# Where the first q is loaded: a GpSimd queue shared by q, k and v, or hardware queues with the cast on VectorE

## The chip, the core and the metric

The kernel runs on one core of a Trainium2 chip. A core has five engines that run side by side, each with its own instruction stream: TensorE (PE, matrix products), VectorE (DVE), ScalarE (ACT), GpSimd (POOL) and SyncE (SP, which here only issues transfers). They meet through semaphores. Data moves between the chip's memory (HBM) and the core's working memory (SBUF) by DMA: an engine issues a transfer, sixteen DMA engines carry it, and a semaphore tells when it has landed. PE writes its results to PSUM, from which DVE or ACT copies them.

The metric is the time of one execution on the device in microseconds (us); lower is better. A profile is one execution with every instruction recorded; its span runs from the first instruction to the last.

## The reference

Linear attention with decay, then a two-layer network with an ELU between. `lam` has one decay per head.

```python
def _attn_ref(q, k, v, lam):                      # q, k, v: (4, 8, 768, 64) float32
    block = 64
    ...
    for b in range(S // block):
        intra = einsum('bhic,bhjc->bhij', qb, kb) * Dmask      # lam ** (i - j), 0 above the diagonal
        intra = einsum('bhij,bhjd->bhid', intra, vb)
        inter = einsum('bhid,bhde->bhie', qb * lam_pow, kv_state)
        out[:, :, sl] = intra + inter
        kv_state = lam_block * kv_state + einsum('bhsd,bhse->bhde', kb * rev_pow, vb)

def _moe_ref(x, w_in, w_out):                     # x: (3072, 512); w_in: 512 x 2048; w_out: 2048 x 512
    h = x @ w_in
    g = where(h > 0, h, exp(min(h, 0)) - 1)
    return g @ w_out
```

## The kernel before

Everything is computed in half precision (FP16) with sums in float. The 3072 tokens are 24 chunks of 128: chunk g is block g // 4 of batch g % 4, so chunks 0 to 3 are the first 128 tokens of the four batches, and they have no earlier state. For a chunk, attention runs over all 8 heads, which are held as 4 pairs (`HP`), two heads of 64 on 128 partitions. The network works on tiles of 4, 2, 4, 4, 4, 4 and 2 chunks (`TS`). The order of the work on each engine is written out by hand; the Tile layer below only adds the semaphores.

**Attention of one chunk.** q and k arrive with tokens on partitions. PE turns them so that the head dimension lies on partitions (`att_T`, L223) and ACT copies the result from PSUM (`att_Te`, L235). PE makes the scores (`att_S`, L310), DVE multiplies them with the decay mask (`att_mask`, L322), PE multiplies with v (`att_O`, L336; for chunk 3 `att_OX2`, L267, in two halves) and ACT copies the result into `xt`, the network's input (`att_X`, L363; `att_OX2`, L272). Later chunks also use and update a state (`att_kd`, `att_U`, `att_st`), with factors `ks`, `up` and `qs`, and with the mask `mask1` in place of `mask`.

**The masks.** `mask` (chunks 0 to 3) is exp(lag x log lam) per head, eight ACT instructions at L172, times a causal matrix (DVE, L175). `mask1` is the causal matrix times `dn` (DVE, L163). ACT loads one table of functions for the logarithm of lam and another for exp.

**The network.** For a tile, `mm1` forms 16 column blocks n of 128 (L443; L461 for tiles of two chunks), ACT makes exp and relu (L472, L476), DVE joins them to `g` (L489, or L484 and L487 for three blocks of the first tile), `mm2` sums over the 16 blocks (L540), and the result is copied and stored (L557; the last chunk by `mm2_last`, L520 to L527). The first tile's stage A is `mm1` with n = 0 to 15, with first `mm2` products between; stage B is the rest of its `mm2`, with attention of chunks 4 and 5 between. From then on the network of one tile and attention of the next are interleaved to the end.

**The loads.** All loads of q, k, v and the weights convert float to half on the way, and are issued by POOL, in the order of the list `LOADS` (`emit_load` L74, `emit_wi` L99, `emit_wo` L106). A load of one chunk's q, k or v writes 128 KB to SBUF, in rows of one token of one head (64 floats in HBM, 64 halves in SBUF). `wi` is loaded in eight pieces of 1, 1, 2, 2, 2, 2, 2 and 4 blocks n, `wo` in five. Two of the entries are no loads but the product `kd` of chunks 0, 1 and 2, 3, which POOL computes (L297) between its issues; it needs `ks`. At most eight of POOL's loads are in flight with one semaphore each: the ninth waits for the first to land. SP issues the load of `lam` (L52), the transposing copies of later chunks (L279) and most stores (L557); those of chunks 18 and 19 are POOL's.

**The opening** (chunks 0 to 3, up to stage A) is the straight list L591 to L645. `warm(k)` (L568) puts in products of ones whose results nobody reads; they keep PE busy while it waits.

Of the kernel before, what the change touches and what calls it, by code (L numbers as in the profile page):

```python
# [7 lines left out]
FP32 = mybir.dt.float32  # L8
FP16 = mybir.dt.float16
I32 = mybir.dt.int32  # L10
AF = mybir.ActivationFunctionType
ALU = mybir.AluOpType
# [3 lines left out]
def kernel(  # L16
# [34 lines left out]
    lam_b = cpool.tile([128, H], FP32, name="lam_b")  # L51
    nc.sync.dma_start(out=lam_b[:], in_=lam.unsqueeze(0).broadcast_to([128, H]))  # L52
    rel_i = cpool.tile([128, 128], I32, name="rel_i")
# [60 lines left out]
    ]  # L114
    LOADS = [(0, 1, 'q'), (0, 1, 'k'), (1, 1, 'q'), (1, 1, 'k'), (2, 1, 'q'), (2, 1, 'k'), (3, 1, 'q'), (3, 1, 'k'), (0, 1, 'v'), (1, 1, 'v'), (2, 1, 'v'), (3, 1, 'v'), ('wi', 0), ('wi', 1), ('wi', 2), ('wi', 3), ('wi', 4), ('kd', 0), ('wi', 5), ('wi', 6), ('wo', 0), ('wi', 7), ('kd', 2), ('wo', 1), ('wo', 2), (4, 2), ('wo', 3), ('wo', 4), (6, 2), (8, 2), (10, 2), (12, 2), (14, 2), (16, 2), (18, 2), (20, 2), (22, 2)]

    def run_loads(items):
        for it in items:
            if it[0] == "wi":
                emit_wi(it[1])  # L120
            elif it[0] == "wo":
                emit_wo(it[1])
            elif it[0] == "kd":
                att_kd(it[1], 2, "p")
            else:
                emit_load(*it)

    run_loads(LOADS[:0])
    nc.gpsimd.iota(rel_i[:], pattern=[[1, 128]], base=0, channel_multiplier=-1)
    run_loads(LOADS[0:16])  # L130

# [27 lines left out]
    dn = cpool.tile([128, H], FP32, name="dn")  # L159
    nc.scalar.activation(dn[:], loglam[:], AF.Exp, scale=pos[:, 0:1])  # L160
    mask1 = cpool.tile([128, 2, HP, 128], FP32, name="mask1")
    for hh in range(2):
        nc.vector.tensor_tensor(  # L163
            out=mask1[:, hh],
            in0=causT[:].unsqueeze(1).broadcast_to([128, HP, 128]),
            in1=dn[:, hh::2].unsqueeze(2).broadcast_to([128, HP, 128]),
            op=ALU.mult,
        )

    def build_mask0(hh):  # L170
        for h in range(hh, H, 2):
            nc.scalar.activation(  # L172
                mask[:, hh, h // 2, :], lag[:], AF.Exp, scale=loglam[:, h : h + 1]
            )
        nc.vector.tensor_tensor(  # L175
            out=mask[:, hh], in0=mask[:, hh],
            in1=causT[:].unsqueeze(1).broadcast_to([128, HP, 128]), op=ALU.mult,
        )

    build_mask0(0)  # L180
    ks = cpool.tile([128, H], FP32, name="ks")
# [27 lines left out]
    def att_T(g, n, which, tag="S"):  # L209

        j = "qk".index(which)
        if n == 1:
            t1 = ps.tile([128, 1, HP, 128], FP16, tag=tag, bufs=2, name=f"psT{which}{g}")
            pT[g, j] = t1[:]
        elif j == 0:
            t2 = ps.tile([128, 2, n, HP, 128], FP16, tag=tag, bufs=2, name=f"psT{g}")
            pT[g, 0], pT[g, 1] = t2[:, 0], t2[:, 1]
        pt = pT[g, j]
        ts = (qn, kn)[j]
        for i in range(n):  # L220
            nat = heads(ts, g + i)
            for hp in range(HP):
                nc.tensor.transpose(  # L223
                    pt[:, i, hp, :], in_=nat[:, 2 * hp : 2 * hp + 2, :],
                    identity=ident16[:],
                )

    def att_Te(g, n, which, eng):
        j = "qk".index(which)
        pt = pT.pop((g, j))  # L230
        dst = asb.tile([128, n, HP, 128], FP16, tag=f"{which}T", name=f"{which}T{g}", bufs=4)
        if eng == "v":
            nc.vector.tensor_copy(dst[:], pt)
        else:
            nc.scalar.copy(out=dst[:], in_=pt)  # L235
        for i in range(n):
            (qT, kT)[j][g + i] = dst[:, i]

    def att_T2(g, which, tag):
# [112 lines left out]
    def att_X(g, n, parts=1):  # L352
        t, i = where[g]
        if i == 0:
            xt[t] = asb.tile([128, HP, TS[t] * L], FP16, tag="xt", name=f"xt{t}")
        po = pS.pop(("O", g))
        w = HP // parts
        for j in range(parts):
            c = slice(j * w, (j + 1) * w)
            dst = xt[t][:, c, i * L : (i + n) * L].rearrange("p h (n l) -> p n h l", n=n)  # L360
            if g < B:
                copy = nc.vector.tensor_copy if g in () else nc.scalar.copy
                copy(out=dst, in_=po[:, :, c])  # L363
                continue
            nc.vector.tensor_tensor(  # L365
                out=dst, in0=po[:, :, c],
                in1=qs[:, c].unsqueeze(1).broadcast_to([128, n, w, 128]),
                op=ALU.mult,
            )

    def att_U(g, tag="S"):
# [160 lines left out]
    def mm2(t, i, n, tag="M"):  # L532
        if T0[t] + i == NG - 1:
            if n == NF - 1:
                mm2_last(t, i)
            return
        if n == 0:
            psM[t, i] = ps.tile([128, DM], FP32, tag=tag, bufs=2, name=f"psM{t}_{i}")
        pm = psM[t, i]
        nc.tensor.matmul(  # L540
            pm[:], lhsT=gt[t][:, n, i * L : (i + 1) * L],
            rhs=wo_t[wo_at[n][0]][:, wo_at[n][1], :], start=(n == 0), stop=(n == NF - 1),
        )
        if n < NF - 1:
            return
        c, b = divmod(T0[t] + i, B)
        t0 = b * S + c * L
        o = msb.tile([128, DM], FP32, tag="osb", bufs=6, name=f"osb{t}_{i}")
        last = T0[t] + i == NG - 1
        if last:  # L550
            raise AssertionError
        else:
            if i % 2:
                nc.vector.tensor_copy(o[:], pm[:])
            else:
                nc.scalar.copy(o[:], pm[:])  # L556
            (nc.gpsimd if T0[t] + i in (18, 19) else nc.sync).dma_start(  # L557
                out=out[t0 : t0 + L, :], in_=o[:]
            )
        psM.pop((t, i))  # L560

    def warm(k, tag="M"):
        if k <= 0:
            return
        pw = ps.tile([128, 4, 128], FP32, tag=tag, bufs=2, name=f"psW{len(warms)}")
        warms.append(pw)
        for w in [4] * (k // 2) + [2] * (k % 2):
            nc.tensor.matmul(  # L568
                pw[:, 0:w], lhsT=ones[:], rhs=any16[:, 0:w], start=True, stop=True
            )  # L570
# [13 lines left out]

    def op_T(c, w):
        att_T(c, 1, w, "H")

    def op_Te(c, w):
        att_Te(c, 1, w, "a")

    W = [14, 6, 2, 2, 2, 0, 2, 0, 4, 0, 0, 2, 0, 2, 0, 0, 4, 0, 0, 0, 0]  # L591
    warm(W[0])
    op_T(0, "q")
    op_Te(0, "q")
    build_mask0(1)
    warm(W[1])
    op_T(0, "k")
    op_Te(0, "k")
    warm(W[2])
    op_T(1, "q")  # L600
    op_Te(1, "q")
    att_S(0)
    att_mask(0, 2)
    warm(W[3])
    op_T(1, "k")
    op_Te(1, "k")
    late_ks()
    warm(W[4])
    op_T(2, "q")
    op_Te(2, "q")  # L610
    att_S(1)
    att_mask(1, 2)
    warm(W[5])
    op_T(2, "k")
    op_Te(2, "k")
    late_up()
    warm(W[6])
    op_T(3, "q")
    op_Te(3, "q")
    att_S(2)  # L620
    att_mask(2, 2)
    late_qs(0, 1)
    warm(W[7])
    op_T(3, "k")
    op_Te(3, "k")
    cut, ecut = {}, {}
    for x, f in zip([('O', 0), ('S', 3), ('qs', 0), ('O', 1), ('qs', 1), ('O', 2), ('qs', 2), ('qs', 3), ('O2', 3, 'S'), ('L', 0, 384)], W[8:]):
        warm(f, "M" if not cut else "S")
        if x[0] == "O":
            att_O(x[1], 1, "M" if x[1] < 2 or not cut else "S")  # L630
            att_X(x[1], 1)
        elif x[0] == "S":
            att_S(x[1])
            att_mask(x[1], 2)
        elif x[0] == "qs":
            late_qs(x[1], x[1] + 1)
        elif x[0] == "O2":
            att_OX2(x[1], x[2])
        elif x[0] == "L":
            lo = cut.get(x[1], 0)  # L640
            mm1_mm(0, x[1], lo, x[2], "M" if x[1] % 2 == 0 else "H")
            cut[x[1]] = x[2]
        elif x[0] == "E":
            elu_cols(0, x[1], 0, cut[x[1]], x[2])
            ecut[x[1]] = cut[x[1]]  # L645

    run_loads(LOADS[16:29])
    for s, g in zip([], (0, 2)):
# [45 lines left out]

    for s, a, b in [(('B', 2), 29, 30), ((1, 2), 30, 31), ((1, 14), 31, 32), ((2, 4), 32, 33), ((2, 12), 33, 34), ((3, 4), 34, 35), ((3, 12), 35, 36), ((4, 4), 36, 37)]:
        at(s, paced_load, s, LOADS[a:b])
# [52 lines left out]
```

## Time and profile before

| | us |
|---|---|
| median of 3 runs (212.57 to 212.66) | 212.57 |
| the profiled execution | 212.6 |
| its span | 210.8 |
| PE busy | 203.6 |
| DVE busy | 148.4 |
| ACT busy | 128.0 |
| POOL busy | 62.4 |
| L540, second matmul, 368 products | 94.0 |
| L443, first matmul, 324 products | 81.4 |

The span is 1.8 us shorter than the execution that it belongs to. A line such as `L443 PE MATMUL psH<-xt,wi` reads: line 443 of the kernel, on PE, writes psH and reads xt and wi. Matmuls overlap in the pipeline, so the time of one alone is longer than the step from one to the next; the step is what counts in a row of them. "PEld" is PE's weight load, which runs beside its products. In a list of the timeline the first number is the start from the span's beginning and the second the length, and what stands in brackets is the idle time before and what ended it. The transfer engines' share counts packets in flight, so it may be over 1. Transfers before, by the page (count, KB written by each, median us from issue to landing):

```profile
qn<-in_q_dram POOLq DMA_DIRECT2D x4, 128.0 KB, 4.5
kn<-in_k_dram POOLq DMA_DIRECT2D x4, 128.0 KB, 4.4
```

### The profile page before, as it was taken

The numbers are of one execution on the slowest core, as the hardware profiler recorded it, in microseconds if no ns is written. First come the engines' busy times: TensorE is split into PE (matmuls) and PEld (weight loads), VectorE is DVE, ScalarE is ACT, GpSimd is POOL, SyncE is SP. The second block draws the span as 40 slices with busy tenths as digits, with TensorE's granted clock in tenths as the row PEclk, the third lists the DMA queues.
The fourth block names the chain that finished last, engine by engine and source line by source line (L and its number), as shares of the span: only waits on it lengthen the run. The fifth ranks groups of instructions, "written<-read, shape, count | busy, mean of one in ns | idle before, by whom it ended". The sixth has DMA issues, their size and how long they took to land.

```text
span 210.8 us, 4132 instructions
## 1 busy us (share of the span) xinstructions
PE 203.6 (97%) x1640; PEld 105.6 (50%) x1640; DVE 148.4 (70%) x241; ACT 128.0 (61%) x247; POOL 62.4 (30%) x71
## 2 busy tenths in 40 slices
PE   6987999999999999999999999999999999999994
PEld 2453444556865454544544544544544544466643
DVE  7774897566989999998697598677557634344321
ACT  6786798307784758666475566475566466675610
POOL 8999985400525160240600600600000000011000
PEclk9999999999999999999999999999999999999999
DMA  5999999999998999998797991799301111011112
GB/s 36 145 155 179 201 195 166 197 157 199 227 145 111 147 153 164 132 106 97 128 151 124 129 122 53 124 147 156 74 0 53 50 50 50 2 53 50 50 53 101
DMA packets 101284, 24.40 MB, mean 116 GB/s; under 512 B 93072, under 2 KB 98448, under 8 KB 101264
## 3 DMA queue, kind: packets, MB, share of 16 engines
q0 software_dynamic: 80912, 14.16, 87.3%
q1 hardware_dynamic: 20208, 9.90, 21.0%
q8 instruction: 13, 0.21, 0.4%
q10 hardware_dynamic: 144, 0.07, 0.1%
q14 instruction: 7, 0.06, 0.1%
HBM read 27.27 MB, written 6.29 MB: 159 GB/s over the span
## 4 chain that ended last, share of the span: by engine, by line
PE 83%; POOL 6%; DMA 3%; DVE 3%; ACT 2%; issue 1%; POOLq 0%; ACTq 0%
PE psM L540 36%; PE psH L443 32%; PE psH L461 5%; DMA wi<-in_moe_w_in_dram 3%; PE psO L336 2%; PE psS L310 2%; PE psO L344 2%; POOL qn L74 2%; POOL kn L74 2%; PE psM L520 2%; POOL vn L74 2%; DVE g L489 1%; PE psU L382 1%; DVE P L322 1%; ACT kd L295 1%
## 5 line engine op out<-in xcount | busy, mean ns | idle before, releaser
L540 PE MATMUL psM<-wo,g 128*128 128x512 f16 x368 | 94.0, 380 | 0.2 <-DVE g L489 0.2
L472 ACT ACTIVATE e<-psH 128x512 f32<-128x512 f32 x96 | 57.4, 598 | 59.8 <-PE psH L443 50.6
L489 DVE SCALAR_TENSOR_TENSOR g<-e,r 128x512 f16<-128x512 f32 x93 | 63.2, 695 | 36.2 <-ACT r L476 35.7
L443 PE MATMUL psH<-xt,wi 128*128 128x512 f16 (+2 forms) x324 | 81.4, 377 | 1.5 <-DMA wi<-in_moe_w_in_dram 1.3
L476 ACT ACTIVATE r<-psH 128x512 f16<-128x512 f32 x93 | 55.2, 594 | 0.0
L540 PEld LDWEIGHTS <-g 128*128 128x128 f16 x368 | 34.3, 98 | 38.5 <-DVE g L489 1.5
L443 PEld LDWEIGHTS <-wi 128*128 128x128 f16 x324 | 31.1, 98 | 39.4 <-DMA wi<-in_moe_w_in_dram 2.0
L322 DVE TENSOR_TENSOR P<-psS,mask 128x1024 f16<-128x1024 f32 (+1 forms) x28 | 28.7, 1067 | 5.3 <-PE psS L310 5.1
L690 POOL COPY pace<-g 1x1 f16<-1x1 f16 x7 | 2.3, 329 | 69.2 <-DVE g L489 69.2
L420 DVE SCALAR_TENSOR_TENSOR st<-st,up_p,psU 64x128 f16<-64x128 f16 x64 | 18.2, 345 | 0.1
L557 POOL DMA_DIRECT2D out_dram<-osb x2 | 1.1, 570 | 54.8 <-ACT osb L556 50.7
L365 DVE TENSOR_TENSOR xt<-psO,qs 128x1024 f16<-128x1024 f32 x10 | 12.2, 1224 | 6.7 <-PE psO L344 6.7
L461 PE MATMUL psH<-xt,wi 128*128 128x256 f16 x128 | 16.4, 273 | 0.0
L74 POOL DMA_DIRECT2D qn<-in_q_dram x14 | 15.4, 1102 | 3.3 <-issue 2.0
L74 POOL DMA_DIRECT2D kn<-in_k_dram x14 | 15.2, 1086 | 1.2 <-DMA kn<-in_k_dram 0.8
L74 POOL DMA_DIRECT2D vn<-in_v_dram x14 | 15.2, 1104 | 1.2 <-DMA wo<-in_moe_w_out_dram 1.1
L556 ACT COPY osb<-psM 128x512 f32<-128x512 f32 x12 | 7.1, 592 | 12.2 <-PE psM L540 12.2
L461 PEld LDWEIGHTS <-wi 128*128 128x128 f16 x128 | 12.4, 98 | 4.2
L336 PEld LDWEIGHTS <-vn 128*64 128x64 f16 x184 | 9.5, 109 | 4.7 <-issue 4.0
L336 PE MATMUL psO<-P,vn 128*64 128x128 f16 x184 | 11.5, 222 | 0.1
L344 PE MATMUL psO<-qT,st 128*64 128x128 f16 x160 | 10.0, 219 | 0.0
L568 PE MATMUL psW<-ones 128*128 128x512 f16 x20 | 8.7, 535 | 1.1 <-DVE ones L55 1.1
(59 smaller groups left out, 118.1 us busy)
## 6 DMA issues: line engine op xcount, KB each, us to landing
out_dram<-osb SPq DMA_DIRECT2D x21, 256.0 KB, 2.5
qn<-in_q_dram POOLq DMA_DIRECT2D x10, 256.0 KB, 7.2
kn<-in_k_dram POOLq DMA_DIRECT2D x10, 256.0 KB, 8.0
vn<-in_v_dram POOLq DMA_DIRECT2D x10, 256.0 KB, 9.0
wo<-in_moe_w_out_dram POOLq DMA_DIRECT2D x3, 512.0 KB, 13.1
wi<-in_moe_w_in_dram POOLq DMA_DIRECT2D x5, 256.0 KB, 7.0
qn<-in_q_dram POOLq DMA_DIRECT2D x4, 128.0 KB, 4.5
kn<-in_k_dram POOLq DMA_DIRECT2D x4, 128.0 KB, 4.4
```

The costliest lines, as they stand in the source:

```text
L74: nc.gpsimd.dma_start(out=dst, in_=src[b : b + n, :, rows].rearrange("b h p d -> p (b h) d"))
L322: nc.vector.tensor_tensor(out=P[:, :, c], in0=s[:, :, c], in1=(mask if g < B else mask1)[:, :, c], op=ALU.mult,)
L336: nc.tensor.matmul(po[r, i, hp, :], lhsT=v_of(g + i, 2 * hp + hh), rhs=P[:, hh, hp, :], start=True, stop=(c == 0), skip_group_check=True,)
L344: nc.tensor.matmul(po[r, i, hp, :], lhsT=st[(g + i) % B // 2][c % 2][:, (g + i) % 2, hp, r], rhs=qT[g + i][:, hp, :], start=False, stop=Tr ...
L365: nc.vector.tensor_tensor(out=dst, in0=po[:, :, c], in1=qs[:, c].unsqueeze(1).broadcast_to([128, n, w, 128]), op=ALU.mult,)
L420: nc.vector.scalar_tensor_tensor(out=new[r, :, hp, r], in0=old[r, :, hp, r], scalar=up_p[r, hp : hp + 1], in1=pu[r, :, hp, :], op0=ALU.mul ...
L443: nc.tensor.matmul(pH[:, lo:hi], lhsT=wi[:, kk, j * 128 : (j + 1) * 128], rhs=xt[t][:, kk, lo:hi], start=(kk == 0), stop=(kk == HP - 1),)
L461: nc.tensor.matmul(pH[:, x * MT : (x + 1) * MT], lhsT=wi[:, kk, j * 128 : (j + 1) * 128], rhs=xt[t][:, kk, :], start=(kk == 0), stop=(kk = ...
L472: nc.scalar.activation(e[:], pH[:], AF.Exp)
L476: nc.scalar.activation(r[:], pH[:], AF.Relu)
L489: nc.vector.scalar_tensor_tensor(out=g, in0=e[:], scalar=-1.0, in1=r[:], op0=ALU.add, op1=ALU.min)
L540: nc.tensor.matmul(pm[:], lhsT=gt[t][:, n, i * L : (i + 1) * L], rhs=wo_t[wo_at[n][0]][:, wo_at[n][1], :], start=(n == 0), stop=(n == NF - 1),
```

## The change

The q of chunks 0 to 3 no longer goes through POOL. It is loaded as float, uncast, by four transfers, two on SP's queue (chunks 0 and 2) and two on ACT's (chunks 1 and 3, behind `lam`, which moves from SP to ACT). Chunks 0 and 1 share one tile `qf`, one on partitions 0 to 63 and the other on 64 to 127; a partition holds two neighbouring tokens of each head, 512 bytes in a row. DVE narrows them to half (`first_qc`, one instruction for the even heads and one for the odd heads of two chunks). PE turns two chunks at a time (`first_qT`, eight products), and ACT's copy out of PSUM (`first_qE`) sorts the tokens back into order. POOL's list then begins with four loads of k and four of v.

The opening is a new list. All 25 half-units of warming (13 products) stand at its head. The mask is finished in two parts by pairs of heads (`decay_caus`), and the scores and their mask product are made in two halves, each with its own PSUM tile (`half_S`, `half_P`). `ks` comes after the third output copy. `mask1` with `dn`, `up` and `qs` leave the opening for stage B. One table of functions for logarithm and exp is loaded ahead. The stores of chunks 16, 17, 20 and 21 move from SP to POOL.

```diff
-    nc.sync.dma_start(out=lam_b[:], in_=lam.unsqueeze(0).broadcast_to([128, H]))
+    nc.scalar.dma_start(out=lam_b[:], in_=lam.unsqueeze(0).broadcast_to([128, H]))
+    qf = [cpool.tile([128, H, 2, 64], FP32, name=f"qf{i}") for i in range(B // 2)]
+    def first_q(b0, e):
+        (nc.sync if e == "s" else nc.scalar).dma_start(
+            out=qf[b0 // 2][b0 % 2 * 64 : b0 % 2 * 64 + 64].rearrange("p h j d -> p h (j d)"),
+            in_=q[b0, :, 0:L].rearrange("h (p j) d -> p h (j d)", j=2),
+        )
+    for b0, e in ((0, 's'), (1, 'a'), (2, 's'), (3, 'a')):
+        first_q(b0, e)
+    nc.scalar.preload_act_table_set("natural_log_exp_and_others")
...
-    LOADS = [(0, 1, 'q'), (0, 1, 'k'), (1, 1, 'q'), (1, 1, 'k'), (2, 1, 'q'), (2, 1, 'k'), (3, 1, 'q'), (3, 1, 'k'), (0, 1, 'v'),
+    LOADS = [(0, 1, 'k'), (1, 1, 'k'), (2, 1, 'k'), (3, 1, 'k'), (0, 1, 'v'),
...
+    def decay_caus(x):
+        c = slice(2 * x, 2 * x + 2)
+        nc.vector.tensor_tensor(out=mask[:, :, c], in0=mask[:, :, c],
+            in1=causT[:].unsqueeze(1).unsqueeze(1).broadcast_to([128, 2, 2, 128]), op=ALU.mult)
...
+    qh = cpool.tile([128, B // 2, HP, 2, 2, 64], FP16, name="qh")
+    qTa = cpool.tile([128, B, HP, 128], FP16, name="qTa")
+    def first_qc(i, hh, eng="v"):
+        (nc.vector.tensor_copy if eng == "v" else nc.scalar.copy)(
+            out=qh[:, i, :, :, hh, :], in_=qf[i][:, hh::2]
+        )
+    def first_qT(i, tag="H"):
+        pTq[i] = ps.tile([128, 2, HP, 2, 64], FP16, tag=tag, bufs=2, name=f"psTq{i}")
+        for hp in range(HP):
+            for j in range(2):
+                nc.tensor.transpose(
+                    pTq[i][:, :, hp, j, :],
+                    in_=qh[:, i, hp, j].rearrange("p a d -> p (a d)"), identity=ident16[:],
+                )
+    def first_qE(g, eng="a"):
+        src = pTq[g // 2][:, g % 2]
+        dst = qTa[:, g].rearrange("p h (t j) -> p h j t", j=2)
+        (nc.vector.tensor_copy if eng == "v" else nc.scalar.copy)(out=dst, in_=src)
+        qT[g] = qTa[:, g]
+    def half_S(g, x, tag="S"):
+        s = ps.tile([128, 2, HP, 128], FP32, tag=tag, bufs=2, name=f"psS{g}_{x}")
+        for y in range(2):
+            hp = 2 * x + y
+            for hh in range(2):
+                r = slice(hh * 64, (hh + 1) * 64)
+                nc.tensor.matmul(
+                    s[:, hh, y, :], lhsT=kT[g][r, hp, :], rhs=qTa[r, g, hp, :],
+                    start=True, stop=True,
+                )
+        pS[g, x] = s
+    def half_P(g, x):
+        if x == 0:
+            Pt[g] = asb.tile([128, 2, HP, 128], FP16, tag="P", name=f"P{g}", bufs=3)
+        c = slice(2 * x, 2 * x + 2)
+        nc.vector.tensor_tensor(
+            out=Pt[g][:, :, c], in0=pS.pop((g, x))[:, :, 0:2], in1=mask[:, :, c], op=ALU.mult
+        )
...
-            (nc.gpsimd if T0[t] + i in (18, 19) else nc.sync).dma_start(
+            (nc.gpsimd if T0[t] + i in (16, 17, 18, 19, 20, 21) else nc.sync).dma_start(
...
+    for op in [('W', 25), ('dn', 0), ('dn', 1), ('dn', 2), ('dn', 3), ('c', 0), ('dn', 4), ('dn', 5), ('dn', 6), ('dn', 7), ('qc', 0, 0), ('qc', 0, 1), ('c', 1), ('Tk', 0, 'H'), ('Ek', 0, 'a'), ('qT', 0), ('qE', 0, 'a'), ('W', 0), ('qc', 1, 0), ('qc', 1, 1), ('Tk', 1, 'H'), ('Ek', 1, 'a'), ('qE', 1, 'a'), ('S', 0, 0), ('P', 0, 0), ('S', 0, 1), ('P', 0, 1), ('Tk', 2, 'H'), ('Ek', 2, 'a'), ('S', 1, 0), ('P', 1, 0), ('qT', 1), ('qE', 2, 'a'), ('qE', 3, 'a'), ('S', 1, 1), ('P', 1, 1), ('Tk', 3, 'H'), ('Ek', 3, 'a'), ('W', 0), ('O', 0, 'M'), ('X', 0, 'a'), ('S', 2, 0), ('P', 2, 0), ('S', 2, 1), ('P', 2, 1), ('W', 0), ('O', 1, 'M'), ('X', 1, 'a'), ('S', 3, 0), ('P', 3, 0), ('S', 3, 1), ('P', 3, 1), ('W', 0), ('O', 2, 'M'), ('X', 2, 'a'), ('ks',), ('OX', 3, 'S'), ('L', 0, 384)]:
+        opening(*op)
+    run_loads(LOADS[10:25])
+    for s, *op in ((('B', 0), 'up'), (('B', 0), 'm1', 0), (('B', 1), 'qs', 0), (('B', 1), 'm1', 1), (('B', 2), 'qs', 1), (('B', 3), 'qs', 2), (('B', 4), 'qs', 3)):
+        at(s, opening, *op)
```

In the list, `Tk` and `Ek` are the turning and copying of k, `dn` the exponentials of the mask, `O` and `X` the products with v and their copies, `OX` both for chunk 3, and `('L', 0, 384)` the first 384 columns of the first tile's block n = 0.

## The prediction

> **What bounds the kernel now.** I read the page's forty slices first, then the chain of waits, then the opening engine by engine. First the busy tenths, each slice 5.27 us:
>
> ```profile
> PE   6987999999999999999999999999999999999994
> POOL 8999985400525160240600600600000000011000
> ```
>
> TensorE (PE) is full from the fifth slice to the last but one. Its windows say so more sharply: 20.00 us busy of the stretch 35 to 55, 119.82 of 75 to 195. From 20 us on there is nothing to gain but what shifts as a whole; the holes are in the first four slices, while GpSimd (POOL) is full. The chain of waits of the first 40 us (start, length, what) says what these holes wait for:
>
> ```profile
> 7.72 0.88 POOL kn L74
> 8.59 3.49 POOL vn L74 x4
> 12.09 1.37 POOL wi L99 x2
> 13.45 6.56 DMA wi<-in_moe_w_in_dram
> 20.01 0.05 issue
> 20.06 4.60 PE psH L443 x20
> ```
>
> POOL issues twelve loads of q, k and v, one after the other, then the weights. The third weight load (columns n = 2 and 3 of the first matmul) is issued at 13.45 and lands at 20.01; PE's second stretch of L443 starts at 20.06 and never stops again. PE did n = 0 and 1 from 16.58 to 18.77 and then stood 1.29 us. So the end is set by **when n = 2 can start**, now 20.06, and two chains lead to it: the loads, and attention of chunks 0 to 3 (16.58, then some 2.0 us for n = 0 and 1). The same loads by stage (stretch; length, busy time of PE, PEld, DVE, ACT, POOL; clock; DMA share, where 1 is 16 engines; GB/s written):
>
> ```profile
> 6.00:10.00 4.00, 3.95 (x26) 1.85 (x24) 2.63 (x5) 3.00 (x9) 4.00 (x5) 1.00 2.35 150
> 10.00:14.00 4.00, 3.29 (x49) 1.94 (x48) 2.99 (x5) 3.73 (x11) 4.00 (x6) 1.00 2.34 149
> 25.00:28.00 3.00, 3.00 (x30) 1.38 (x28) 2.95 (x5) 2.26 (x6) 3.00 (x4) 1.00 1.24 206
> 32.00:35.00 3.00, 3.00 (x16) 1.35 (x15) 2.65 (x5) 2.58 (x6) 1.38 (x2) 1.00 2.43 159
> ```
>
> A q, k or v load writes 128 KB; POOL issues one each 0.87 us, which is 150 GB/s, just what the engines moved from 6 to 14 us. From 32 to 35, with q and k loads waiting in the queue, they moved 159. So POOL and the transfer engines are at their limits together, 0.87 and about 0.83 us per load.
>
> **The change: the loads.** Four of POOL's first eight issues go. v then starts where the fifth slot began, 5.09 instead of 8.59: every later issue is **3.50 us** earlier. The ninth load needs the first one's semaphore back, long landed. That is the upper bound. The bytes of q still pass the same 16 engines, now as 1 MB of 512-byte rows from the hardware queues. No row shows such a load. Bounds: weights in 2 KB rows, 206 GB/s written, thus 412 read, give 2.5 us; q as now, 302 read, 3.5. I take 3.0, since the rows lie between. They can start at about 2.0: the small load of lam, issued at 0.74, landed 2.55 us later and its first data must come before. Then 3.0 for q and 8 x 0.83 for k and v end at 11.6, with some 0.9 to the semaphore (k of chunk 3 landed 4.5 us after its issue) 12.5; by POOL's slots the eighth load lands at 12.2 as it does now. The last v lands now at 15.8 (issued 11.12, 4.7 to landing), so the gain is 3.3, with 3.5 us for q 2.8. The weights behind it keep their distance, 4.2 us to the third: it lands at 16.7, bounds 16.5 and 17.2.
>
> The Trainium skill, "DMA: Bandwidth & Descriptors", section "Rules for kernel authors", speaks against the change: spreading loads over queues does not help, because all run on the same engines, and only issue time is saved. The row it meets is POOL's 4.00 of 4.00. By the rule, with the engines as the limit, the sum would be that of the third rival below.
>
> **The opening's compute.** VectorE (DVE) carries the most. Its clears end at 4.95 as now (rows L158). Removed ahead of the first mask product: two products of mask1 (2 x 0.61), moved to stage B. The decay masks still take two products. ScalarE (ACT) now issues three loads first (0.37 each, as its one issue at the end), so its one table load runs 1.9 to 3.2; the second table load (1.28) and the decay dn leave. lam lands at 3.3, eight exponentials of 0.29 end at 5.9, the first four at 4.7. Added: four narrowings of 128x512 from float to half on DVE. Their nearest rows are three (L484):
>
> ```profile
> 21.76 1.10 DVE L484 TENSOR_SCALAR m<-e 128x512 f16<-128x512 f32 x1 [1.01 <-ACT e L472]
> ...
> 24.10 0.42 DVE L484 TENSOR_SCALAR m<-e 128x512 f16<-128x512 f32 x1
> ...
> 25.76 0.91 DVE L484 TENSOR_SCALAR m<-e 128x512 f16<-128x512 f32 x1
> ```
>
> The same work took 0.42, 0.91 and 1.10 us; during each of them POOL was busy. With POOL issuing without pause in the opening I take 0.70 a step, bounds 0.45 and 1.10. So on DVE: mask half to 5.56, two narrowings to 6.96 (q of chunks 0 and 1 landed by about 5), mask half to 7.57, two narrowings to 8.97. PE's eight transposes, ACT's two copies (0.48 a step) and the first scores take 6.96 to about 8.6, beside the rest. Eight mask products of 0.61 without a hole run 9.0 to 13.9; now they run 9.12 to 15.64 with holes for k and q. Then 0.3 to PE, 0.35 for chunk 3's values, n = 0 from 14.5, and n = 2 could start at **16.6**; at 0.45 a narrowing 15.8, at 1.10 18.2. Copies on ACT: as many as before, four for k and four for q.
>
> POOL may in turn be held by the narrowings: its issue at 23.96 beside the 0.42 one took 1.31 against 1.15 of its neighbours, 0.16 more; four make 0.6, and the third weight load 17.3. The Trainium skill, "SBUF — State Buffer", section "Who interferes with whom", is harsher: such a copy takes the port that DVE and GpSimd share, and the other waits for the whole instruction. By it four copies of 0.42 cost POOL 1.7 us, the weights come at 18.4, and the sum is 210.9.
>
> **The sum.** n = 2 starts at the later of 16.7 (16.5 to 17.8) and 16.6 (15.8 to 18.2). Both are uncertain and the later one counts, so I take **16.95**, a gain of 3.1 us.
>
> **What is moved, and its cover.** ks comes after the third output copy, about 13.9 on ACT. POOL's product kd waits for it and holds five weight loads and what follows. POOL reaches it at 12.2 and ends it at 16.0; the next weight load lands 6.5 later (as now: 17.52 to 24.02), at 22.5, and n = 8, which reads it, starts 5.9 after n = 2, at 22.8. It costs nothing, but only 0.3 is left: if ks is later than n = 2 by more, PE stops there. Up, dn, qs (2.2 us of ACT) and mask1 (1.2 of DVE) go to stage B, where ACT is busy 9.01 of 20 us and DVE 13.61 (35 to 55); nothing. The stores of chunks 16, 17, 20 and 21 go from SP to POOL: 0.57 each, with POOL idle and no load queued behind; nothing. The 20 warming matmuls become 13 in one piece up front; what this may cost is a rival below.
>
> The profiled run took 212.6 with a span of 210.8; the median is 212.57. 212.6 - 3.1 = **209.5 us**, its own range 208.9 to 210.9.
>
> **Rivals.** (1) *PE stays slow.* The warming rows show a step of 0.43 us for 512 columns until 9.8 and 0.22 later:
>
> ```profile
> 1.06 3.17 PE L568 MATMUL psW<-ones 128*128 128x512 f16 x7 [1.06 <-DVE ones L55]
> ...
> 9.01 0.61 PE L568 MATMUL psW<-ones 128*128 128x512 f16 x1
> ```
>
> So PE came to speed after 8.7 us of nearly unbroken work. Now it works 5.3 us (to 6.4) and then in small pieces. If these don't count, the first matmul starts slow at 14.5 and each us of it loses half. Until 7 us of slowness it ends below the old time; nine lose 4.5: n = 2 is at 21.0 instead of 16.5, **213.5**. Against it: at the slow step the opening's pieces take twice as long, some 6.6 of the 8 us, as dense as what worked now. 0.18, of which 0.13 slower and 0.04 level. (2) *The shared port*: narrowings of 1.10 make attention the last, n = 2 at 18.2: **210.7**. For it: two of three rows. 0.17. (3) *q is only moved*: the transfers alone are the limit. Then only q's start counts, 2.0 against 3.1 (the first q landed at 4.9, less 0.9 and 0.87), and 3.0 for q instead of 4 x 0.85: 1.5 us, **211.1**. For it: the DMA share of 2.35, and that the weight loads queue; against it the engines' 69 GB/s from 2 to 6 us, half of 150. 0.12. (4) *The forecast*, 0.53.
>
> **Chances.** Faster by over 0.2% (0.43 us, about what a measurement of this kernel can tell from no change): 0.53 + 0.17 + 0.12 + 0.01 = 0.83; within 0.04; slower 0.13. The range 208.9 to 212.3 leaves out the best corner (0.05) and the slow clock's upper part (0.14).
>
> **What would show it.** Right: POOL's first v issue near 5.1 and third weight load near 10; it lands at 16.5 to 17.3; the last mask product ends near 14; the second stretch of the first matmul (L512 of the changed kernel) starts at 16.6 to 17.2 and PE has no hole later. Wrong: narrowings at 1.1, the step of 0.43 beyond 14 us, q landing after 6, PE waiting for weights at n = 8, or PE holes in stage B.

## The result, and the profile after

The changed kernel took **218.44 us** (median of 4 runs, 217.42 to 219.9) against 212.57 for the kernel before: a ratio of 1.0281, 95% interval 1.0222 to 1.0341. It is 5.9 us slower, where 3.1 us faster was forecast. The profiled run took 219.9 with a span of 218.1, 7.3 us more than the span before, and it is this difference that the traces are compared by.

All but 0.4 of it has arisen by 35 us. The first product of block n = 10 starts at 34.93, where it was at 28.03; from there on the products of both matmuls are 6.9 us late to the end. The remaining 0.4 lies behind the last product, which ends at 214.74 (before 207.87), but not in the stores: the last one lands 1.9 us after it, as before (2.0). From the last product to the end of the span it is 3.4 us instead of 3.0; in the kernels with q by POOL below it is 3.1. What the program waits for there was not taken apart. PE's timeline of the changed kernel (start, length, line, tile, count; in brackets the idle time before and what ended it):

```profile
1.06 4.93 PE L637 MATMUL psW<-ones 128*128 128x512 f16 x13 [1.06 <-DVE ones L66]
11.09 0.61 PE L238 MATMUL psTk<-ident,kn 128*128 128x128 f16 x4 [5.11 <-DMA kn<-in_k_dram]
...
20.70 6.12 PE L512 MATMUL psH<-xt,wi 128*128 128x384 f16 x28
28.98 1.74 PE L512 MATMUL psH<-xt,wi 128*128 128x512 f16 x4 [2.15 <-DVE g L556]
```

There are two holes that the kernel before didn't have: 5.11 us for the first k, and 2.15 us in the middle of the first matmul. The first work of any length in the chain of waits of the changed kernel (start, length, what) is the first of them:

```profile
1.39 9.65 DMA kn<-in_k_dram
```

The first k is issued at 1.39, as POOL's first load always was, and needs 9.65 us; the same slot took 3.5 us before (q, landed at 4.92). The transfer view of the stretch 2 to 10 us shows who had the engines (packets, MB, share of 16 engines; then KB each and median us from issue to landing):

```profile
q0 software_dynamic: 2093, 0.27, 62.4%
q10 hardware_dynamic: 1173, 0.53, 44.0%
q1 hardware_dynamic: 1056, 0.52, 33.9%
...
kn<-in_k_dram POOLq DMA_DIRECT2D x4, 128.0 KB, 9.1
qf<-in_q_dram SPq DMA_DIRECT2D x1, 256.0 KB, 6.9
```

The two hardware queues (q10, q1) moved q's 1.05 MB in these 8 us; POOL's queue (q0) wrote 0.27 MB, though eight of its loads, 1.05 MB in SBUF, had been issued by 8.8. The same view of 2 to 5.5 us has no line for POOL's queue at all:

```profile
q1 hardware_dynamic: 654, 0.33, 42.4%
q10 hardware_dynamic: 619, 0.26, 39.4%
```

POOL's first packet started at 5.6, where it had started at 3.1; q's packets ran from 2.3 to 9.6. The hardware loads landed at 5.56, 6.92, 8.46 and 10.70, on average one each 1.7 us ((10.70 - 5.56) / 3); the first k at 11.05, right behind the last of them, and the other seven at POOL's usual pace, up to 16.79 (5.74 / 7 = 0.82 us each). Twelve loads were through at 15.81 before; now eight are through 1.0 us later.

The windows show what the first hole did to PE's clock (stretch; length, busy time of PE, PEld, DVE, ACT, POOL; granted clock, the share of its full clock that PE ran at; DMA share; GB/s):

```profile
5.00:10.00 5.00, 0.99 (x5) 0.22 (x3) 2.41 (x4) 1.69 (x6) 3.79 (x5) 0.87 1.80 169
10.00:15.00 5.00, 3.49 (x34) 2.67 (x35) 1.96 (x4) 2.84 (x5) 3.54 (x5) 0.50 3.00 149
15.00:20.00 5.00, 4.80 (x60) 3.29 (x60) 3.66 (x7) 3.00 (x6) 0.18 (x1) 0.50 1.85 184
```

The granted clock falls to half at 8.7 us, 2.7 us after the last warming product ended (1.06 + 4.93 = 5.99), and stays there until 22.3: the attention of chunks 0 to 3 is computed in a dense chain at half speed (four transposes 0.61 us, 0.40 at full clock). The Trainium skill, "TensorE: Matmul & The Clock Gate", section "Why this matters for your kernels", warns of idle gaps of more than some 3 us. The first hole, 5.11 us, is such a gap; but the second, of 2.15 us, was enough as well (the clock fell at 29.1), so there the measurement is stricter than the page. The runs give no fixed length: a hole of 2.65 us in the kernel with q by POOL below left the clock at 1.00.

The second hole begins with POOL. Its timeline:

```profile
11.33 3.85 POOL L110 DMA_DIRECT2D wi<-in_moe_w_in_dram  x5 [2.54 <-DMA kn<-in_k_dram]
20.93 1.90 POOL L358 TENSOR_TENSOR kd<-kn,ks 128x1024 f16<-128x1024 f16 x1 [5.75 <-ACT ks L202]
22.78 1.55 POOL L110 DMA_DIRECT2D wi<-in_moe_w_in_dram  x2
...
25.79 2.13 POOL L358 TENSOR_TENSOR kd<-kn,ks 128x1024 f16<-128x1024 f16 x1
```

The ninth load waited 2.54 us for the first k's semaphore, so that the weights were issued only 0.65 us earlier than before. Then POOL stood 5.75 us for `ks`, which the opening's order places behind the third output copy (20.5 on ACT), and did its next eight pieces without a pause, just as DVE began on the first matmul:

```profile
23.66 2.50 DVE L558 SCALAR_TENSOR_TENSOR g<-e,r 128x512 f16<-128x512 f32 x2 [2.52 <-ACT r L545]
26.09 2.12 DVE L553 TENSOR_SCALAR m<-e 128x512 f16<-128x512 f32 x1
...
29.45 0.42 DVE L553 TENSOR_SCALAR m<-e 128x512 f16<-128x512 f32 x1
```

L553 takes 0.42 us at 29.45, where POOL only issues a load; here it took 2.12, the length of POOL's second `kd` from 25.79 to 27.92, and the first of the two L558, from 23.67, took 1.90 instead of 0.68 beside POOL's issues. DVE frees the PSUM tiles that late, and PE waits.

The sum for the profiled run: n = 2 starts at 23.21 instead of 20.06, 3.15; the hole 2.15; the rest to 6.9, 1.6, is PE at half clock once more, from 29.1 to 32.5 after the second hole (half of 3.4 is 1.7); 0.4 at the end.

### The profile page after: what moved, and what is told of

The parts are those of the page before. It is cut to its first block, busy times and chain, and to the rows that moved or that the text cites. A ratio compares the mean times of both kernels' runs of the same rounds, so it can differ in the third digit from the quotient of the medians.

```text
span 218.1 us, 4123 instructions
## 1 busy us (share of the span) xinstructions
PE 205.5 (94%) x1633; PEld 107.8 (49%) x1633; DVE 151.7 (70%) x245; ACT 127.2 (58%) x245; POOL 61.5 (28%) x71
## 4 chain that ended last, share of the span: by engine, by line
PE 84%; DVE 6%; DMA 4%; ACT 3%; issue 1%; POOL 0%; POOLq 0%; ACTq 0%
PE psM L609 35%; PE psH L512 31%; PE psH L530 5%; DMA kn<-in_k_dram 4%; PE psO L397 3%; DVE g L558 2%; PE psS L371 2%; PE psO L405 2%; PE psM L589 2%; PE psU L451 1%; DVE P L383 1%; ACT r L545 1%; ACT kd L356 1%; PE psS L286 1%; DVE m L553 1%
## 5 line engine op out<-in xcount | busy, mean ns | idle before, releaser
L558 DVE SCALAR_TENSOR_TENSOR g<-e,r 128x512 f16<-128x512 f32 x93 | 64.0, 700 | 38.3 <-ACT r L545 37.9
L512 PE MATMUL psH<-xt,wi 128*128 128x512 f16 (+2 forms) x324 | 83.2, 385 | 2.3 <-DVE g L556 2.2
L512 PEld LDWEIGHTS <-wi 128*128 128x128 f16 x324 | 31.9, 100 | 40.9 <-issue 4.6
L383 DVE TENSOR_TENSOR P<-psS,mask 128x1024 f16<-128x1024 f32 x20 | 23.5, 1218 | 2.2 <-PE psS L371 2.1
L626 POOL DMA_DIRECT2D out_dram<-osb x6 | 3.3, 551 | 62.8 <-ACT osb L625 48.6
L489 DVE SCALAR_TENSOR_TENSOR st<-st,up_p,psU 64x128 f16<-64x128 f16 x64 | 18.2, 346 | 0.1
L426 DVE TENSOR_TENSOR xt<-psO,qs 128x1024 f16<-128x1024 f32 x10 | 12.2, 1224 | 6.8 <-PE psO L405 6.8
L530 PEld LDWEIGHTS <-wi 128*128 128x128 f16 x128 | 12.3, 98 | 4.2
L85 POOL DMA_DIRECT2D qn<-in_q_dram x10 | 11.6, 1162 | 2.9 <-issue 1.7
L397 PE MATMUL psO<-P,vn 128*64 128x128 f16 x184 | 12.2, 234 | 0.0
L405 PEld LDWEIGHTS <-st 128*64 128x64 f16 x160 | 8.9, 110 | 0.0
```

Of the source, the lines that this page charges most:

```text
L85: nc.gpsimd.dma_start(out=dst, in_=src[b : b + n, :, rows].rearrange("b h p d -> p (b h) d"))
L383: nc.vector.tensor_tensor(out=P[:, :, c], in0=s[:, :, c], in1=(mask if g < B else mask1)[:, :, c], op=ALU.mult,)
L397: nc.tensor.matmul(po[r, i, hp, :], lhsT=v_of(g + i, 2 * hp + hh), rhs=P[:, hh, hp, :], start=True, stop=(c == 0), skip_group_check=True,)
L405: nc.tensor.matmul(po[r, i, hp, :], lhsT=st[(g + i) % B // 2][c % 2][:, (g + i) % 2, hp, r], rhs=qT[g + i][:, hp, :], start=False, stop=Tr ...
L426: nc.vector.tensor_tensor(out=dst, in0=po[:, :, c], in1=qs[:, c].unsqueeze(1).broadcast_to([128, n, w, 128]), op=ALU.mult,)
L489: nc.vector.scalar_tensor_tensor(out=new[r, :, hp, r], in0=old[r, :, hp, r], scalar=up_p[r, hp : hp + 1], in1=pu[r, :, hp, :], op0=ALU.mul ...
```

## Experiments

Theory at the start: the hardware loads of q hold back POOL's loads; this late start, the late `ks` and the slow clock then add up. Rivals: one of the two latter does it alone, or the number of rows, not the bytes, makes the hardware loads slow.

**What comes on top: ks and the clock.** Three kernels, all else as in the changed kernel. First `ks` early:

```diff
-... ('dn', 7), ('qc', 0, 0), ... ('X', 2, 'a'), ('ks',), ('OX', 3, 'S'), ...
+... ('dn', 7), ('ks',), ('qc', 0, 0), ... ('X', 2, 'a'), ('OX', 3, 'S'), ...
```

> The changed kernel with ks moved up, right behind the eight exponentials of the mask on ACT (which then stands idle until 11.7). Theory 'late q and k': the first k lands at 11.05 because four hardware loads of q hold the transfers, and this alone costs the 3.3 us by which n = 2 starts late (23.3 against 20.06); ks adds a second loss of its own, POOL's 5.7 us wait, which puts its second product kd beside DVE's ELU (m took 2.1 us, PE stood 2.15 us, then ran slow from 29.0 to 32.4). By it POOL computes kd at about 15, weight load 6 lands near 23 instead of 26.7, the hole at 26.8 goes, n = 2 stays at 23.3: 214.5 to 216.5. Rival 'clock alone': PE is slow in any case and ks matters little: 217.5 to 219.5.

Then `('W', 25)` made `('W', 72)`, 36 warming products:

> The changed kernel with 36 instead of 12.5 warming products at its head, so that PE works until the first k lands at about 11. Theory 'late q and k': k still lands at 11 and v of chunk 3 at 16.8, so n = 0 cannot start before 17.2; the quick clock saves the 2 to 3 us that PE's small pieces lose (n = 0 at 17.5 to 18.5 instead of 20.7), n = 2 at 20 to 21, behind before's 20.06; the hole from kd remains: 214 to 216. Rival 'clock alone': with the clock open the change brings what was forecast, 209.5 to 211.

Then both:

> Both of the two edits: ks behind the mask's exponentials and 36 warming products. Theory 'late q and k': what is left is the late landing alone, n = 2 at 19.5 to 20.5 (third weight load at 19.0): 211.5 to 213.5, level with before. Rival 'the halves are too slow': compute keeps n = 2 beyond 21.5 though all has landed: over 214.

| | time, us | ratio to before | first k lands | n = 2 | hole after it | n = 7 |
|---|---|---|---|---|---|---|
| before | 212.58 | | 6.80 | 20.06 | none | 24.96 |
| changed | 218.44 | 1.0281 | 11.05 | 23.21 | 2.15 | 31.22 |
| ks early | 214.99 | 1.0121 [1.0067, 1.0174] | 10.84 | 23.40 | 0.17 | 28.51 |
| 36 warming products | 218.09 | 1.0264 [1.0230, 1.0299] | 10.68 | 20.77 | 2.65 | 29.41 |
| both | 214.22 | 1.0068 [1.0046, 1.0091] | 10.94 | 20.29 | 0.40 | 25.63 |

With `ks` early POOL does its first `kd` at 15.62 and the hole is all but gone: the late `ks` is worth 3.4 us. Warming alone brings n = 2 forward by 2.4 us, but runs into the same hole, so that its time missed the 214 to 216 expected; the rival "clock alone" missed by far more. With both, n = 2 was where the theory had put it, the time was not: 1.6 us of the loss remain, with the first k still at 11. Neither of the two is the whole cause, and neither repair makes a gain. Note what remains: n = 2 is late by 0.23 only, the hole costs 0.40, the last product is 1.0 late (208.91), and 0.4 lies behind it. The late k thus takes away the gain that was forecast; of the 5.9 us lost beyond that, `ks` and the clock are 4.2.

**What the hardware loads do to POOL's.** In the kernel before, with nothing else changed, the loads of q were added on the hardware queues, into tiles that nobody reads, ahead of everything:

```diff
+    qx = [cpool.tile([128, H, 128], FP32, name=f"qx{i}") for i in range(2)]
+    for i in range(4):
+        (nc.scalar if i % 2 else nc.sync).dma_start(
+            out=qx[i * 64 // 128][i * 64 % 128 : i * 64 % 128 + 64],
+            in_=q[i, :, 0:L].rearrange("h (p j) d -> p h (j d)", j=2),
+        )
```

> The kernel before with the four hardware loads of q added to it (two tokens to a row, 512 rows of 512 bytes each, two on SP's queue behind lam, two on ACT's); nobody reads them. Theory 'hardware loads hold POOL's loads back': the first q of POOL, now landing at 4.9, lands at 10 or later though POOL issues it at the same time, and the run is some 4 to 6 us longer than before. Rival 'they share': POOL's first loads land 1 to 2 us later, all of it made up by the third weight load; the time within 1 us of before.

The same with eight tokens to a row (`j=8`, 2 KB rows on 16 partitions):

> The same with the same bytes in 128 rows of 2 KB for each load (eight tokens to a row, 16 partitions). Theory 'rows': the four loads are done by about 4 and POOL's first load lands at 5 to 6; the time within 1 us of before. Rival 'bytes': as with the rows of 512 bytes.

With one token of one head to a row, on all partitions:

> The kernel before with 1 MB of q loaded besides through hardware queues, unread, now one token of one head per row (256 bytes, 4096 rows, all 128 partitions; the same megabyte in 512-byte rows on 64 partitions landed at 10.79 us and POOL's first load, issued at 1.39, at 10.45). Theory 'descriptors' (the hardware queues make so many rows per us, some 250, whatever their length): twice the rows, last landing near 19, POOL's first load near 18, time 226 to 228. Theory 'partitions' (the slowness comes from writing to few partitions, as 16 partitions were slower than 64): last landing at 6 to 8, POOL's first load by 7, time 214 to 216. Theory 'bytes' (any megabyte takes the same 8.5 us): landings as with 512 bytes, 10.5 to 11, time 218.

With 1 MB of the second weight matrix in place of q:

> The kernel before with 1 MB of the second weight matrix loaded besides through hardware queues, unread: four loads of 128 rows of 2 KB on 128 partitions. 'Descriptors': 512 rows in all, last landing by 5, POOL's first load by 6, time 213 to 214. 'Partitions': the same 6 to 8 as for 256-byte rows on 128 partitions, POOL's first load by 7, time 214 to 216. 'Bytes': 10.5 to 11, POOL's first load near 10.5, time 218.

With only the first of the four loads:

> The kernel before with only one of the four unread hardware loads (256 KB of q in 512-byte rows on 64 partitions, SP's queue). If POOL's first load waits until the hardware loads issued ahead of it are through, it follows this one's end, near 5 to 6 us, instead of 4.92 without and 10.45 with four, and the time is 212.6 to 214. If the bytes share the engines from the start, POOL's first load lands at 4.92 plus a quarter of the 5.53 that four cost, 6.3, with the same time. If a hardware load at all sets POOL's queue back by a fixed time, POOL's first load is near 10 again and the time 217 to 218.

| hardware loads added to the kernel before | these land at | POOL's first load lands | POOL's twelfth load lands | twelfth later by, for each 256 KB | last product ends | time, us |
|---|---|---|---|---|---|---|
| none | | 4.92 | 15.81 | | 207.87 | 212.6 |
| one, 512-byte rows, 64 partitions | 5.27 | 5.91 | 16.10 | 0.3 | 207.86 | 213.5 |
| four, 2 KB rows of a weight, 128 partitions | 5.16 to 7.22 | 8.18 | 18.14 | 0.6 | 210.23 | 215.91 |
| four, 512-byte rows, 64 partitions | 5.51 to 10.79 | 10.45 | 20.23 | 1.1 | 212.89 | 218.23 |
| four, 256-byte rows, 128 partitions | 6.21 to 10.10 | 10.83 | 20.65 | 1.2 | 213.28 | 218.45 |
| four, 2 KB rows, 16 partitions | 6.81 to 12.70 | 13.13 | 23.00 | 1.8 | 215.60 | 221.22 |

The waits of PE in the kernel with four loads in 512-byte rows, where q by POOL is issued at 1.39 as ever (us in total, times, longest):

```profile
PE psTq L229 <- DMA qn<-in_q_dram: 6.3, 1, 6.3
```

So four hardware loads of q alone, with the old opening and the old `ks`, cost 5.6 us. That this is nearly the time of the changed kernel (218.44) is in part chance: here POOL still loads q as well, twelve loads behind the hardware ones instead of eight, and there the late `ks` comes on top. POOL's first load lands about when the hardware loads ahead of it are through, and moves with their number: neither a fixed delay nor an unrelated wait. Rows were refuted twice: twice as many rows (256 bytes) end at about the same time, and a quarter as many on 16 partitions end later. What does make a difference is long rows over all partitions, 7.22, but q's layout doesn't offer them: a token of a head is 256 bytes, and more tokens to a row means fewer partitions. What counts for the price is the twelfth load, behind which the weights queue: four loads of q put it off by 1.1 to 1.8 us for each 256 KB, more than the 0.87 that a slot of POOL's is worth, the weight's long rows by 0.6. The slots won by taking all four q from POOL are thus overpaid in every shape of q that was tried.

For one load this does not hold. It puts off POOL's first landing by 1.0 us, but the twelfth by 0.3, and the third weight load lands at 19.49, earlier than before (20.01). PE's last products, before and with the one load:

```profile
204.22 3.66 PE L520 MATMUL psM<-wo,g 128*128 128x384 f16 x32
204.21 3.66 PE L524 MATMUL psM<-wo,g 128*128 128x384 f16 x32
```

They end at the same time; what this kernel takes longer, 0.8 us in the profiled runs, lies behind them, at the program's end (3.8 us instead of 3.0), and the other times of the table have 0.6 to 0.9 us of that in them too. The engines had room for one load: from 2 to 6 us they move 69 GB/s in the kernel before, half of the 150 later. Whether moving one or two of the four q to a hardware queue would gain was not tried.

In the changed kernel itself four tokens to a row (1 KB, 32 partitions) were tried as well; the narrowing, the turning and ACT's copies follow the layout:

```diff
-            in_=q[b0, :, 0:L].rearrange("h (p j) d -> p h (j d)", j=2),
+            in_=q[b0, :, 0:L].rearrange("h (p j) d -> p h (j d)", j=4),
```

> The changed kernel with four tokens to a row of q instead of two: 256 rows of 1 KB to a load instead of 512 of 512 bytes, the same bytes, queues and number of loads; narrowing, turning and ACT's copies follow the new layout (eight copies of 256 columns for four of 512). ks and the warming stand as in the changed kernel. Theory 'rows': the hardware queues deliver some 270 rows a us whatever their size, so the last q lands at about 6.5 instead of 10.7, the first k near 7, the third weight load at 16 to 17; with ks still late: 212.5 to 215. Rival 'bytes': 1 MB takes its 7 us whatever the rows; last q beyond 9.5, first k beyond 10, the time 217 to 219.

219.18 us (1.0298 [1.0271, 1.0326]): the last q landed at 8.90 and the first k at 9.82, earlier than with two tokens, but far from 6.5. The time didn't follow: in this layout all four q must have landed before the first turning, and the copies out of PSUM became the chain's next link. As a test of the rows it is mixed; the kernels with unread loads keep the rows apart from the rest.

**Order of issue, or precedence?** The four unread loads, all on SP, behind a small DVE write so that they are issued at 2.78 to 4.92:

```diff
+    for i in range(2):
+        nc.vector.memset(qx[i][:, 0, 0:1], 0.0)
+    for i in range(4):
+        nc.sync.dma_start(
...
```

> The kernel before with the same four unread hardware loads of q (512-byte rows, 1 MB), now all on SP's queue and issued from about 4 us on, when POOL has issued three or four loads of its own; POOL's first four landings without them are 4.92, 6.80, 7.76 and 8.57, the eighth 12.20. If the transfer engines work in order of issue, the first three stay within 0.5 us and only those issued later are late. If hardware loads go first whenever they are issued, POOL's second to fourth loads wait until they are through, near 11 to 14. If the two share the engines alike, POOL's loads take about twice as long from 5.5 us on: the second near 8, the fourth near 11. In each case the megabyte has to pass before the third weight load: 216 to 219 us.

PE's timeline of this kernel, as far as it waits for POOL's loads:

```profile
5.02 0.61 PE L231 MATMUL psTq<-ident,qn 128*128 128x128 f16 x4 [0.79 <-DMA qn<-in_q_dram]
...
8.38 0.61 PE L231 MATMUL psTk<-ident,kn 128*128 128x128 f16 x4 [1.47 <-DMA kn<-in_k_dram]
...
11.04 0.61 PE L231 MATMUL psTq<-ident,qn 128*128 128x128 f16 x4 [1.64 <-DMA qn<-in_q_dram]
...
14.56 0.61 PE L231 MATMUL psTk<-ident,kn 128*128 128x128 f16 x4 [1.82 <-DMA kn<-in_k_dram]
```

POOL's first load is untouched (4.97). The second was issued at 2.44, ahead of every hardware load, and lands at 8.33 instead of 6.80; the third at 11.00 instead of 7.76, the fourth at 14.51 instead of 8.57. The hardware loads land at 8.79, 10.63, 12.22 and 14.16, one each 1.8 us, on average the pace that they have when they go first (there with gaps of 1.3, 1.4 and 2.6 us). None of the three expectations fits whole: order of issue is refuted by the second and third load, full precedence by the second's 8.33, even sharing by the fourth. What the run shows is that side by side POOL's loads slow down far more than the hardware loads, to about one in 3 us instead of 0.87, whichever was issued first. Why they share like this stays open. 218.33 us (1.0270 [1.0240, 1.0300]).

**The same opening without hardware loads.** q goes back to POOL in the new layout, cast on the way, ahead of k; the narrowings stay as copies from half to half, so that the order of the work is that of the changed kernel:

```diff
-    qf = [cpool.tile([128, H, 2, 64], FP32, name=f"qf{i}") for i in range(B // 2)]
+    qf = [cpool.tile([128, H, 2, 64], FP16, name=f"qf{i}") for i in range(B // 2)]
-        (nc.sync if e == "s" else nc.scalar).dma_start(
+        nc.gpsimd.dma_start(
-    LOADS = [(0, 1, 'k'), (1, 1, 'k'), ...
+    LOADS = [('q', 0), ('q', 1), ('q', 2), ('q', 3), (0, 1, 'k'), (1, 1, 'k'), ...
```

> The changed kernel, but the four loads of q are issued by POOL ahead of k, cast on the way into a half-precision tile of the same layout; the narrowings on DVE stay as copies from half to half. Only the path of q is undone. Theory 'hardware loads hold the others back': q lands by 8.6, k from 9.5 to 12.2 as the slots of the kernel before, v of chunk 3 at 15.8, third weight load at 20; PE still has a hole of 3 us before k and the late ks: 215 to 218, but the fifth slot lands at 9.5 and the 12 loads keep 0.87 us between landings. Rival 'the path does not matter': first landing of k at 11 or later in this kernel too.

215.87 us (1.0157 [1.0110, 1.0204]). The first k lands at 8.93 behind four loads of q, 2.1 us *earlier* than with q on the hardware queues, and n = 2 starts at 19.80. The hole for `ks` is still there (2.65). With `ks` early and 54 half-units of warming besides:

> All repairs at once: q of chunks 0 to 3 by POOL with the cast on the way (two tokens to a row, ahead of k), ks behind the mask's exponentials, 27 warming products so that PE works until the first k lands near 8.9. Theory 'late q and k, late ks, slow clock' are the three losses and nothing else is wrong with the opening by halves: n = 2 at 19 to 20 with no hole behind it, 211.5 to 212.8. Rival 'the halves cost something of their own': over 213.5.

213.06 us (1.0006 [0.9974, 1.0038]), level with the kernel before and between the two expectations. n = 2 starts at 19.12, 0.9 earlier than before, and a hole of 1.00 us follows. DVE's timeline there, with POOL's second `kd` at 19.78 to 22.02:

```profile
20.55 2.02 DVE L558 SCALAR_TENSOR_TENSOR g<-e,r 128x512 f16<-128x512 f32 x1 [0.29 <-ACT r L545]
```

The second `kd` moved ahead, behind the sixth weight load:

```diff
-    ... ('kd', 0), ('wi', 5), ('wi', 6), ('wo', 0), ('wi', 7), ('kd', 2), ...
+    ... ('kd', 0), ('wi', 5), ('kd', 2), ('wi', 6), ('wo', 0), ('wi', 7), ...
```

> The kernel with q by the GpSimd queue, ks early and 54 half-units of warming (213.06, level with before; its n = 2 starts 0.7 us earlier than before, but a hole of 1.00 us follows at 22.74, when DVE's L558 took 2.02 us beside POOL's second product kd at 19.78), with that second kd put right behind the sixth weight load, so that POOL does it at 17.5 to 19.6, ahead of DVE's work on the first matmul. If POOL's product holds DVE, the hole goes (under 0.2), weight loads land as before since they queue, and the time is 211.7 to 212.2, faster than before by 0.2 to 0.4%. If the hole has another cause, or the product now holds weight loads or mask products, the time is 212.8 to 214.

213.13 us (1.0016 [1.0004, 1.0027]). PE's timeline:

```profile
18.99 4.49 PE L512 MATMUL psH<-xt,wi 128*128 128x512 f16 x20 [0.69 <-DMA wi<-in_moe_w_in_dram]
...
37.59 0.62 PE L238 MATMUL psT<-ident,kn 128*128 128x128 f16 x8 [1.23 <-DMA kn<-in_k_dram]
```

The hole is gone, as it should be if POOL's product holds DVE (it now meets only one L558, from 18.59, which took 1.56 us), and n = 7 starts at 23.78, 1.2 us ahead of the kernel before. But the time is not the 211.7 to 212.2 expected: the gain is given back at 37.59, where PE waits 1.23 us for k of chunks 4 and 5. POOL issued this load 1.0 us earlier than before (24.25, 25.27), and it landed 0.9 later (37.55, 36.65); why was not taken apart. No version was found that beats the kernel before.

## Why the prediction was wrong

**The step that failed** is the price of q's hardware load: "weights in 2 KB rows, 206 GB/s written, thus 412 read, give 2.5 us; q as now, 302 read, 3.5. I take 3.0". Both bounds are rows of POOL's own queue, read as if the sixteen engines had one speed for every queue and shape. Its packets took 7.4 us, from 2.3 to 9.6, and the last load landed at 10.70; no row of before had a hardware load of this size, and the bounds from POOL's loads didn't bound it. They also count bytes read from HBM, twice those written where a load casts. By bytes written, as the rows' GB/s are, q's 1.05 MB uncast would have been 5.1 and 7.0 us (1.05 / 0.206, 1.05 / 0.150), much nearer; that this is what sets the time was not tested. With it went the assumption that k and v follow at 0.83 each right behind: their pace was right (0.82), their start over 4 us off (the eighth was forecast at 12.2 to 12.5 and landed at 16.79).

**POOL's slots, 3.50 us earlier**: true for the issues (the first v at 5.06), not for the landings. "The ninth load needs the first one's semaphore back, long landed" became 2.54 us of waiting. The third weight load landed at 18.96, forecast 16.7; by then it was no longer what n = 2 waited for.

**The opening's compute**: forecast to begin turning by 6.96 and to reach n = 0 at 14.5. It began at 11.09 and reached n = 0 at 20.70. The length of the chain was right, its start and its clock were not: forecast 7.5 us, the chain from the first k to n = 0 is 9.6 us long at half clock and 7.6 at full (10.94 to 18.55 in the kernel with `ks` early and warming), so a first k near 7 would have been needed. Of the narrowings, two took 0.43 and 0.79 beside an issue of POOL's, which took 1.13 instead of 0.90, and two 0.43 and 0.42 while POOL stood; 0.70 was chosen. So the second rival, the shared port, was wrong about its place. But the rule behind it, in the Trainium skill, "SBUF — State Buffer", section "Who interferes with whom", is seen at work at 26.09 us: L553 took 2.12 for 0.42 and ended 0.3 us behind POOL's product.

**"It costs nothing, but only 0.3 is left" (ks)**: the condition came true. ACT made `ks` at 20.5 instead of 13.9, POOL stood 5.75 us, and undoing this one edit is worth 3.4 us, more than half the loss. The cover that the step named was too thin to be priced at nothing. It was priced as a wait of PE for weights at n = 8; it came earlier, as DVE held by POOL.

**Rival 1, PE stays slow**, came true in mechanism, but for another reason than the one given: not that work in small pieces doesn't count, but that PE stood 5.11 us for k. Its 213.5 left out that PE's start is itself late. **Rival 3, q is only moved**, had the right kind of answer, that q's bytes pass the same engines, and by far too small a price: four hardware loads put POOL's twelfth load off by 1.1 to 1.8 us each in q's layouts, more than the slot of 0.87 that each frees. Its point that q can start while the engines have room holds for one load (0.3), not for four. The forecast's own range, 208.9 to 210.9, is a little wider than its bounds for n = 2 give (16.5 and 18.2: 209.0 and 210.7).

**Right**: nothing in stage B and later costs anything (up, dn, qs and mask1: PE has no new wait after 35 us); the stores on POOL cost at most 0.15 behind the last product (3.1 us to the end instead of 3.0 in the kernels with q by POOL, which have these stores too).

## What to carry to other kernels

Before a load is moved to another queue, ask what bounds it: where the page shows the transfer engines as busy as the queue that issues, freeing issue slots gains little, and the moved bytes may go slower in their new shape. What fits into a stretch in which the engines have room can be nearly free: here one load, not four. Take the price of a load from a row with the same queue, row length and number of partitions, or measure it first by adding it, unread, to the kernel as it is: that is one run, and here it alone would have shown that there is no gain: 5.6 us added (218.23 against 212.6), while four freed slots can bring 3.5 at most. Read the price off where it counts, at the loads that PE waits for and at the last product, not at the first landing: by the first landing one load costs 1.0 us, by the last product nothing. Where a step "costs nothing" with 0.3 us to spare, carry the case in which its cover is late as a term of its own.

## What the runs showed of the hardware

- Loads from two queues that run beside each other don't share alike: behind POOL's first load, hardware loads of q landed one each 1.8 us for 256 KB, while POOL's fell from one in 0.87 us to one in about 3. Issued around POOL's first load instead, they kept its packets out until 5.6 us (3.1 without them).
- One hardware load of 256 KB in front of twelve POOL loads put off the first by 1.0 us, the twelfth by 0.3 and PE's last product by nothing; four put off the twelfth by 4.4.
- For the same megabyte, the last hardware load landed at 7.22 (2 KB rows, 128 partitions), 10.10 (256 bytes, 128), 10.79 (512 bytes, 64) and 12.70 us (2 KB rows, 16). The share of the row length and that of the partitions were not separated.
- POOL's issues of q in rows of two tokens followed each other in some 0.68 us, those of rows of one in 0.87.
- Holes of PE of 2.15 and 2.65 us were followed by half clock in two kernels (the changed one, and that with 36 warming products), one of 2.65 us in a third was not.
